# A decode block on one core: w1 in one transfer, w2 in four pieces in place of three

## The chip, the cores and the metric

The kernel runs on one core of a Trainium2 chip. The metric is device time in microseconds (us); lower is better. The core has five engines that run side by side: PE (TensorE, matrix products; PEld is its weight loads), DVE (VectorE), ACT (ScalarE), POOL (GpSimd), and SP (SyncE), which here only issues transfers. The transfers are carried out by 16 DMA engines, and an engine that needs a transfer's data waits until all of it has landed.

## The reference

One token (B = 1, S = 1, D = 640) passes a transformer block whose layer norms are scaled, shifted and gated by a conditioning vector c. All arrays are float32.

```python
mod = silu(c) @ w_mod                      # six vectors of 640: sa, ca, ga, sb, cb, gb
h = layernorm(x) * (1 + ca) + sa
q = h @ wq                                 # 32 heads of 192
p = softmax(q k^T * 192**-0.5)             # k_cache: 32 heads x 8192 x 192
x = x + ga * ((p @ v_cache) @ wo)
h = layernorm(x) * (1 + cb) + sb
f = relu(h @ w1 + b1) ** 2                 # w1: 640 x 1536
x = x + gb * (f @ w2 + b2)                 # w2: 1536 x 640
```

The two caches make up nearly all of the bytes read; w1 and w2 are 3840 KB each.

## The kernel before

Everything big goes through one ring of three equal slots in the on-chip memory (`slot`, L97). In turn they hold a first bundle of small weights (wm0), then the chunks of the caches with wq and wo packed between them (`PLAN`, L50 to L85), and at the end three bundles of weights, each in a slot of its own: wm1 (the modulation weights for the second half), w1 and w2. `load(n)` (L206) asks for slot number n, and SP issues the transfers for it; SP waits at that place in its queue until the last reader of the slot's former content is done. The order of the instructions on each engine is that of the program text; no scheduler moves them.

The loop over the chunks (L363) multiplies keys by the query on DVE (L258), adds halves on POOL (L385), reduces to scores on DVE (L266), takes the softmax, and multiplies the values on PE (L307). At the end of each pass `load(n + 3)` (L410) asks for the slot that this chunk leaves. The last three passes so ask for wm1, w1 and w2. The slot for w2 is the one that the last chunk leaves; its last reader is the matmul of `attend` at L342.

How a bundle is cut into transfers is told by lists of column positions, one transfer from each to the next (L213 to L220):

```python
W1_CUT = (3 * FF, KB * FF)            # L44: blocks 0-2, 3-4 of 5
W2_CUT = (6 * D, 10 * D, 12 * D)      # L45: blocks 0-5, 6-9, 10-11 of 12
...
            for b in cuts:            # L218
                nc.sync.dma_start(chunk_t[n][:, a:b], src[:, a:b])
                a = b
```

A block of w1 is 32 rows of each of four groups of rows (1536 columns, 768 KB); there are KB = 5. A block of w2 is the same of w2 (640 columns, 320 KB); there are FB = 12. A transfer is a wait of its own: a matmul waits for the piece that holds its block.

After the loop come, in this order: the last heads' attention (L417 to L420); the modulation vectors from wm1 (`mod`, L183) with the gathering of the attention's result (`gather`, L347) between its blocks; the second layer norm on DVE and ACT, with the matmuls of the last gate (`gate`, L187; L194) put between its steps on PE; the transpose of its result to hT2 (L123, called at L432); the first product over the five blocks of w1:

```python
    for b in range(KB):               # L436
        for g in range(G):
            nc.tensor.matmul(pf[32 * g:32 * (g + 1), :FG], hT2[:, b], w1_t[:, b, FG * g:FG * (g + 1)],
                             start=(b == 0), stop=(b == KB - 1))
```

then bias, relu and square on DVE (L441 to L443) and their transpose to fT (L123, called at L444), two small DVE operations for the gated bias (L447, L448), the second product, of the same form, over the 12 blocks of w2 (L453), and on DVE the gate and the residual (L456, L457). SP stores the result (L458). In the trace every matmul of L438 and L453 shows as two instructions with a weight load each: 8 instructions for a block, 40 for w1, 96 for w2.

Of the kernel before, what the change touches and what calls it, by code (L numbers as in the profile page):

```python
# [14 lines left out]
D = 640  # L15
# [3 lines left out]
FF = 1536  # L19
# [3 lines left out]
KB = DG // 32  # L23
# [17 lines left out]
VPC = 5  # L41
LEAD_FROM = 1300
LEAD = 120
W1_CUT = (3 * FF, KB * FF)  # L44
W2_CUT = (6 * D, 10 * D, 12 * D)  # L45
WM_CUT = (KB * D + 9 * D, KB * D + 15 * D)
EPS = 1e-5

# [40 lines left out]
def block_kernel(ctx: ExitStack, tc: tile.TileContext, kv, wm0, wm1, w1, w2, out):  # L89
# [7 lines left out]
    def slot(name):  # L97
        return strm.tile([P, SLOT], F32, tag="slot", name=name, bufs=3)
# [107 lines left out]
    def load(n):  # L206
# [5 lines left out]
        else:  # L212
            name, src, cuts = (("wm1_t", wm1, WM_CUT), ("w1_t", w1, W1_CUT), ("w2_t", w2, W2_CUT))[n - len(PLAN)]  # L213
            chunk_t[name] = slot(name)
# [286 lines left out]
```

## Time and profile before

| what | value |
|---|---|
| median of three runs | 1055.79 us (1055.74 to 1055.89) |
| the profiled execution | 1055.83 us |
| its span, first to last instruction | 1054.0 us |
| busy: DVE, PE, POOL, ACT | 830.2, 497.1, 188.2, 43.5 us |
| read from memory | 451.8 MB, 429 GB/s over the span |
| mean granted clock of PE | 0.718 of full speed |
| w1, two transfers: size, time from issue to landing | 2304 KB, 20.5 us; 1536 KB, 23.8 us |
| w2, three transfers: size, time from issue to landing | 1920 KB, 16.6 us; 1280 KB, 19.2 us; 640 KB, 20.3 us |

The times are read from the start of the span. What lies around the span (1.8 us) is start and end of the program. A time from issue to landing contains the time behind the transfers that were queued before. Idle time in the profile is put down to what ended it, written as `<-` and the engine, tile and line waited for.

### The profile page before, as it was taken

The numbers are of one execution on the slowest core, as the hardware profiler recorded it, in microseconds if no ns is written. First come the engines' busy times: TensorE is split into PE (matmuls) and PEld (weight loads), VectorE is DVE, ScalarE is ACT, GpSimd is POOL, SyncE is SP. The second block draws the span as 40 slices with busy tenths as digits, with TensorE's granted clock in tenths as the row PEclk, the third lists the DMA queues.
The fourth block names the chain that finished last, engine by engine and source line by source line (L and its number), as shares of the span: only waits on it lengthen the run. The fifth ranks groups of instructions, "written<-read, shape, count | busy, mean of one in ns | idle before, by whom it ended". The sixth has DMA issues, their size and how long they took to land.

```text
span 1054.0 us, 5116 instructions
## 1 busy us (share of the span) xinstructions
PE 497.1 (47%) x2100; PEld 133.9 (13%) x2100; DVE 830.2 (79%) x428; ACT 43.5 (4%) x122; POOL 188.2 (18%) x57
## 2 busy tenths in 40 slices
PE   2253345565452364535354357344436346345286
PEld 1010011111110010101011011011001011011022
DVE  1798878877959969888797895999887977988822
ACT  1000000000000000000000000000000000000001
POOL 0212121121212202212121121122211211211200
PEclk9676576778666686668676577676677767768699
DMA  9999999999999999999999999999999999999997
GB/s 408 434 429 431 429 432 443 449 428 431 429 433 431 429 436 430 433 430 442 435 430 433 433 427 430 436 439 436 429 429 433 432 436 438 434 431 430 420 428 313
DMA packets 8960, 452.15 MB, mean 429 GB/s; under 512 B 997, under 2 KB 1001, under 8 KB 1129
## 3 DMA queue, kind: packets, MB, share of 16 engines
q1 hardware_dynamic: 8936, 451.83, 99.3%
q8 instruction: 16, 0.26, 0.1%
q14 instruction: 8, 0.06, 0.0%
HBM read 451.82 MB, written 0.00 MB: 429 GB/s over the span
## 4 chain that ended last, share of the span: by engine, by line
DMA 56%; DVE 30%; PE 12%; ACT 1%; issue 0%; SPq 0%; DVEq 0%
DMA chunk<-in_kv 53%; DVE chunk L258 16%; DVE sc L266 12%; PE ps_o L307 6%; PE ps_q L239 2%; DMA w_t<-in_w 2%; PE att_a L340 2%; DMA wm_t<-in_wm 1%; DVE os L321 1%; DVE om L319 1%; PE ps_mod L183 0%; PE att_a L342 0%; ACT p L290 0%; PE ps_mx L282 0%; DVE nm L284 0%
## 5 line engine op out<-in xcount | busy, mean ns | idle before, releaser
L258 DVE TENSOR_TENSOR chunk<-chunk,qb 128x8064 f32<-128x8064 f32 (+19 forms) x81 | 419.7, 5212 | 127.8 <-DMA chunk<-in_kv 122.5
L307 PE MATMUL ps_o<-chunk,p 128*32 128x512 f32 x1536 | 301.5, 747 | 70.3 <-DMA chunk<-in_kv 60.8
L266 DVE TENSOR_REDUCE sc<-chunk 128x25 f32<-128x4800 f32 (+21 forms) x109 | 333.9, 3097 | 0.4
L385 POOL TENSOR_TENSOR chunk<-chunk 128x1824 f32<-128x1824 f32 (+9 forms) x51 | 187.5, 3676 | 806.5 <-DVE chunk L258 578.5
L282 PE MATMUL ps_mx<-ident,mp 128*128 128x128 f32 x32 | 14.5, 452 | 346.8 <-DVE mp L280 346.8
L307 PEld LDWEIGHTS ps_o<-chunk,p 128*32 128x32 f32 x1536 | 68.2, 133 | 278.6 <-issue 193.1
L340 PE MATMUL att_a<-chunk,oT 128*32 128x512 f32 x96 | 65.1, 833 | 42.6 <-DVE oT L330 42.6
L239 PE MATMUL ps_q<-chunk,ln_h 128*128 128x512 f32 x110 | 66.6, 767 | 25.8 <-DMA chunk<-in_kv 25.8
L282 PEld LDWEIGHTS ps_mx<-ident,mp 128*128 128x128 f32 x32 | 5.6, 176 | 375.6 <-DVE mp L280 306.8
L290 ACT ACTIVATE p<-sc,nm 128x256 f32<-128x256 f32 x32 | 16.2, 508 | 649.6 <-DVE nm L284 649.6
L239 PEld LDWEIGHTS ps_q<-chunk,ln_h 128*128 128x128 f32 x110 | 26.7, 253 | 63.7 <-issue 34.6
L319 DVE TENSOR_TENSOR om<-ps_o,mask 96x512 f32<-96x512 f32 x32 | 21.6, 675 | 8.5 <-PE ps_o L307 8.5
L284 DVE TENSOR_REDUCE nm<-ps_mx 128x1 f32<-128x128 f32 x32 | 9.3, 292 | 19.5 <-PE ps_mx L282 19.5
L321 DVE TENSOR_REDUCE os<-om 96x64 f32<-96x512 f32 x32 | 21.8, 682 | 1.1
L340 PEld LDWEIGHTS att_a<-chunk,oT 128*32 128x32 f32 x96 | 12.2, 142 | 78.1 <-DVE oT L330 45.1
L329 DVE TENSOR_REDUCE oT<-ps_oT 128x3 f32<-128x96 f32 x16 | 4.0, 248 | 21.0 <-PE ps_oT L325 21.0
L295 PE MATMUL ps_sum<-ident,wide 128*128 128x128 f32 x16 | 7.4, 465 | 22.4 <-ACT wide L293 22.4
L183 PE MATMUL ps_mod<-wm_t,silu 128*32 128x320 f32 (+1 forms) x80 | 9.4, 621 | 15.8 <-DVE silu L171 15.7
L325 PE MATMUL ps_oT<-ident,os 96*128 96x96 f32 x16 | 5.0, 313 | 20.8 <-DVE os L321 20.8
L342 PE MATMUL att_a<-chunk,oW 128*96 128x384 f32 x32 | 14.6, 538 | 0.0
L240 ACT ACTIVATE qb<-ps_q 128x512 f32<-128x512 f32 x12 | 7.2, 597 | 137.2 <-PE ps_q L239 137.2
L338 ACT ACTIVATE oW<-oT 128x96 f32<-128x96 f32 x16 | 4.5, 280 | 177.6 <-DVE oT L330 177.6
(78 smaller groups left out, 93.6 us busy)
## 6 DMA issues: line engine op xcount, KB each, us to landing
chunk<-in_kv SPq DMA_DIRECT2D x38, 8064.0 KB, 37.2
chunk<-in_kv SPq DMA_DIRECT2D x11, 8000.0 KB, 39.0
chunk<-in_kv SPq DMA_DIRECT2D x2, 7872.0 KB, 38.5
chunk<-in_kv SPq DMA_DIRECT2D x1, 6144.0 KB, 27.9
wm_t<-in_wm SPq DMA_DIRECT2D x1, 4493.5 KB, 13.9
wm_t<-in_wm SPq DMA_DIRECT2D x1, 4480.0 KB, 27.6
chunk<-in_kv SPq DMA_DIRECT2D x1, 3264.0 KB
chunk<-in_kv SPq DMA_DIRECT2D x1, 3072.0 KB, 28.2
```

The costliest lines, as they stand in the source:

```text
L183: nc.tensor.matmul(ps[32 * g:32 * (g + 1), :n * DG], e[:, b:b + 1].to_broadcast([P, 32]), wb[:, :, DG * g:DG * (g + 1)], start=(b == 0), s ...
L239: nc.tensor.matmul(ps, h1[:, b:b + 1].to_broadcast([P, P]), w[:, b], start=(b == 0), stop=(b == KB - 1))
L258: nc.vector.tensor_mul(pr, pr, q[:, None, :].to_broadcast([P, b - a, DH]))
L266: nc.vector.tensor_reduce(sc[:, a % SRING:a % SRING + b - a], src[:, a - first:b - first], axis=AX.X, op=ALU.add)
L282: nc.tensor.transpose(ps[:, :P], mp.to_broadcast([P, P]), ident)
L290: nc.scalar.activation(p, s[:, :, None].to_broadcast([P, NPOS, 32 // E]), AF.Exp, bias=nm, accum_out=sp[:, h % 2:h % 2 + 1])
L307: nc.tensor.matmul(ps_t[h][32 * g:32 * (g + 1)], p[:, E * j:E * (j + 1)].rearrange("p e r -> p (e r)"), t[:, g], start=(j == 0), stop=last)
L319: nc.vector.tensor_mul(om[:n], ps_t.pop(h)[:n].rearrange("p (d e) -> p d e", e=E), mask[:n, None, :].to_broadcast([n, ED, E]))
L321: nc.vector.tensor_reduce(os_[:n, h % 2], om[:n], axis=AX.X, op=ALU.add)
L340: nc.tensor.matmul(att_a[96:, :512], oT[:, j:j + 1].to_broadcast([P, 32]), w[:, j, :512], start=(first and j == 0), stop=(last and j == NV ...
L342: nc.tensor.matmul(att_a[:96, :NV * (D - 512)], oW.rearrange("p j r -> p (j r)"), w[:, :, 512:], start=first, stop=last)
L385: nc.gpsimd.tensor_add(half, half, kt[:, m:, DH // 2:])
```

## The change

Two lists of cuts change and nothing else. w1 comes in one transfer of five blocks (3840 KB) in place of three and two blocks. w2 comes in four transfers, of six, three, two and one block (1920, 960, 640 and 320 KB), in place of six, four and two. The order of the bytes in the queue stays as it was, and so does the number of transfers, five.

```diff
-W1_CUT = (3 * FF, KB * FF)
-W2_CUT = (6 * D, 10 * D, 12 * D)
+W1_CUT = (KB * FF,)
+W2_CUT = (6 * D, 9 * D, 11 * D, 12 * D)
```

## The prediction

> **What bounds the kernel now.** I read the page first, for what runs all the time. Rows two and three of this fence are the busy share of the DMA engines and what they moved, in 40 slices of 26 us; the last is the chain of work that ended last, by engine.
>
> ```profile
> span 1054.0 us, 5116 instructions
> ...
> DMA  9999999999999999999999999999999999999997
> GB/s 408 434 429 431 429 432 443 449 428 431 429 433 431 429 436 430 433 430 442 435 430 433 433 427 430 436 439 436 429 429 433 432 436 438 434 431 430 420 428 313
> ...
> DMA 56%; DVE 30%; PE 12%; ACT 1%; issue 0%; SPq 0%; DVEq 0%
> ```
>
> The DMA engines are at nine tenths in every slice but the last. The kernel is a stream of bytes, and the change neither adds nor removes a byte. So only the end of the stream can matter, and I go to the chain in order of time there (start, us, what).
>
> ```profile
> 1027.86 0.83 PE att_a L342 x2
> 1028.69 0.02 issue
> 1028.71 0.33 SPq L219
> 1029.04 0.05 issue
> 1029.09 0.43 SPq L219
> 1029.51 0.05 issue
> 1029.56 20.33 DMA w_t<-in_w
> 1049.89 0.04 issue
> 1049.93 0.80 PE ps_y L453 x16
> 1050.73 0.02 issue
> 1050.75 0.34 DVE y L456
> 1051.11 0.33 DVE y L457
> ```
>
> The slot for w2 comes free when L342 has read its last chunk; SP then issues the three pieces of w2, and the last of them lands at 1049.89. From there 0.04 us pass to the first matmul that uses it, 16 matmuls follow (two blocks), then two DVE operations and the store. **The landing of the last byte sets the end**, and 0.84 us lie between it and L456. Next, the timeline of the last steps (start, us, engine, line, tiles, count, and in brackets the idle time before with what ended it).
>
> ```profile
> 1036.97 1.30 PE L194 MATMUL ps_mod<-wm_t,silu 128*64 128x320 f32 x8
> ...
> 1038.49 0.34 DVE L123 STREAM_TRANSPOSE hT<-ln_h 128x160 f32<-128x160 f32 x1
> 1038.91 0.19 PEld L438 LDWEIGHTS ps_f<-w_t,hT 128*32 128x32 f32 x8 [1.20 <-PE ps_mod L194]
> 1038.94 3.43 PE L438 MATMUL ps_f<-w_t,hT 128*32 128x384 f32 x40 [0.67 <-PE ps_mod L194]
> ...
> 1040.71 0.32 PEld L438 LDWEIGHTS ps_f<-w_t,hT 128*32 128x32 f32 x8 [0.32 <-DMA w_t<-in_w]
> ...
> 1042.43 0.56 DVE L441 TENSOR_TENSOR f<-ps_f,bbt 128x384 f32<-128x384 f32 x1 [3.59 <-PE ps_f L438]
> ...
> 1044.01 0.58 DVE L123 STREAM_TRANSPOSE fT<-f 128x384 f32<-128x384 f32 x1
> ...
> 1044.83 0.33 DVE L448 TENSOR_TENSOR x<-x,gb 128x160 f32<-128x160 f32 x1
> 1045.37 1.54 PEld L453 LDWEIGHTS ps_y<-w_t,fT 128*32 128x32 f32 x48 [3.70 <-issue]
> 1045.40 1.84 PE L453 MATMUL ps_y<-w_t,fT 128*32 128x160 f32 x48 [3.03 <-DMA w_t<-in_w]
> 1048.38 0.97 PEld L453 LDWEIGHTS ps_y<-w_t,fT 128*32 128x32 f32 x32 [1.46 <-DMA w_t<-in_w]
> 1048.38 1.29 PE L453 MATMUL ps_y<-w_t,fT 128*32 128x160 f32 x32 [1.14 <-DMA w_t<-in_w]
> 1049.93 0.43 PEld L453 LDWEIGHTS ps_y<-w_t,fT 128*32 128x32 f32 x16 [0.58 <-DMA w_t<-in_w]
> 1049.93 0.75 PE L453 MATMUL ps_y<-w_t,fT 128*32 128x160 f32 x16 [0.26 <-DMA w_t<-in_w]
> ```
>
> A block of w2 is 8 matmuls here (48 for six). All three pieces of w2 are waited for, so PE has time to spare there. The second piece of w1 is waited for by a weight load at 1040.71, but the row of the matmuls is one run without a gap: that wait costs nothing today.
>
> **The change part by part.**
>
> *Issue.* SP issues one transfer less for w1 and one more for w2. The first is worth nothing, because SP then waits for L342 until 1028.71 anyway. The second comes at about 1030.0, one step of 0.43 + 0.05 us behind the last of before. Its cover is w1: in the order of the queue w2's bytes come only when w1's are in, at 1040.7. Without that 10 us cover it would cost 0.48 us.
>
> *Bytes.* PE's restarts tell when pieces land: 1280 KB take 1048.38 - 1045.37 = 3.01 us, 640 KB take 1049.93 - 1048.38 = 1.55 us. So 640 KB more cost 1.46 us (2.28 us per 1000 KB), and 1.55 - 1.46 = 0.09 us is the price of a transfer as such. Three blocks (960 KB) then take 2.28 us, and one block (320 KB) 0.82 us. The lower end for one block is half of the 1.55 us (0.78), the upper end the whole 1.55, as if size no longer counted. I take 0.82, near the lower end, since 1280 to 640 KB nearly halved. w2's tail becomes 2.28 + 1.55 + 0.82 = 4.65 us in place of 4.56, and w1 gives the same 0.09 back for its removed transfer: the last byte stays at 1049.89, and the pieces are usable at about 1045.37, 1047.65, 1049.2 and 1049.93. The transfers number five as before, so the waits at the kernel's end do not grow.
>
> The Trainium skill's page "DMA: Bandwidth & Descriptors", section "Bandwidth", speaks against such cuts: make transfers of at least 1 MiB to reach three quarters of the peak. Here 640 KB came in 1.55 us, 423 GB/s against 435 for the 1280 KB, so the trace does not bear it out behind a full queue.
>
> *The wait for w1.* L438 starts on a whole w1. The weight load that waits today goes at 1040.71, and 0.03 us later matmuls start (1038.91 to 1038.94 is the same step now), so 1040.74 in place of 1038.94: **1.80 us later**. Behind it on PE stand only L438's and L453's matmuls; behind L438 stand DVE's f, its square and its transpose. The 3.43 us of matmuls end at 1044.17, and fT is ready at 1044.59 + 1.80 = 1046.39. L447 and L448, next on DVE, end at 1046.96 in place of 1045.16, and L457 needs them at about 1051: hidden with 4 us to spare. From DVE's end to PE's first matmul I take 0.2 us, a little above the nearest step (fT's twin before L438, whose transpose of 0.34 us starts at 1038.49: 0.11 us); 0.1 would be the lower end, 0.5 a generous upper one. L453 starts at 1046.6 instead of 1045.40. This is the price of the edit, and it falls into the 1.84 us of work followed by 1.14 us of idle that L453 has today.
>
> *The pace of L453.* Four matmuls run side by side. From 16 to 48 matmuls the run grows from 0.75 to 1.84 us: 1.09 us for 8 groups of four, 0.136 a group, and a block is two groups. From 1046.6, blocks 0 to 5 take until 1048.23 (three blocks are there since 1047.65, no wait), blocks 6 to 8 until 1049.05 (wait to 1049.2), blocks 9 and 10 until 1049.77, and **the last block starts when it lands, 1049.93**. PE has caught up with 0.16 us in hand.
>
> *The end.* Behind the last landing stands one block in place of two: 0.75 - 2 x 0.136 = 0.48 us. That is 0.27 us less, and L456, L457 and the store move with it. Nothing else is late.
>
> **Sum:** the profiled execution took 1055.83 us (span 1054.0 and 1.83 us around it), less 0.27 is 1055.56. It lies 0.04 us over the median of 1055.79, so the forecast is **1055.5 us**, 0.03% less. That is far inside 0.2% (2.1 us), about what a measurement of this kernel can tell from no change. By its own unknowns: if the last piece came 0.16 us or more earlier, PE would be the bound and the gain 0.43 (1055.4); if one block took 1.55 us, the end is 0.73 later (1056.25).
>
> **The rivals.**
>
> *Slower: the clock of PE falls in the new gap.* PE now rests from the end of L194 to L438 and again from there to L453. These are stretches of this execution (window, its length, busy time and count of PE, PEld, DVE, ACT, POOL, then granted clock, DMA share, GB/s):
>
> ```profile
> 968.60:982.60 14.00, 0.48 (x1) 0.18 (x1) 11.99 (x5) 0.60 (x2) 4.04 (x1) 0.63 0.99 429
> 982.60:985.60 3.00, 2.95 (x12) 0.77 (x15) 2.97 (x1) 0.00 (x0) 0.00 (x0) 0.50 1.02 441
> ...
> 1042.40:1045.40 3.00, 0.00 (x0) 0.03 (x1) 2.59 (x6) 0.00 (x0) 0.00 (x0) 1.00 0.99 416
> 1045.40:1047.30 1.90, 1.84 (x48) 1.52 (x48) 0.00 (x0) 0.00 (x0) 0.00 (x0) 1.00 0.62 254
> ```
>
> After 14 us with 0.48 us of work the clock was at half for at least the next 3 us of work; after 3.0 us with none it was full. The new gaps are 1038.27 to 1040.74 (2.5 us) and 1044.17 to 1046.6 (2.4 us), both shorter than the one that did no harm, so this is unlikely. If it came, L438's 3.43 us would double, L453 would start at 1050.0, and its 24 groups (23 x 0.136 + 0.35 = 3.5 us) would end at 1053.5 where now 1050.68 stands: **1058.6 us**. It decides as soon as PE is over 0.16 us late. The Trainium skill's page "TensorE: Matmul & The Clock Gate", section "Why this matters for your kernels", advises against rests over about 3 us between bursts; by it the old gap was at the edge and the new ones are under it, which agrees with the rows.
>
> *Small transfers have a price that the old sizes hide.* One block takes the 1.55 us of two: **1056.25 us**. The fence on L453 speaks against it, as 1280 and 640 KB scale; below 640 KB no row of w2 shows it. The Trainium skill's page "DMA: Bandwidth & Descriptors", named above, points this way.
>
> *PE becomes the bound.* If L453's start is 0.3 to 0.9 us later than reckoned, the catching up fails, and 0.14 to 0.74 of it is seen: **1055.7 to 1056.25 us**. Then the change does not do what it says: the last cut no longer decides.
>
> *The latest DMA engine changes.* The 16 engines do not finish together; the windows, with DMA share and GB/s as their last columns:
>
> ```profile
> 1040.00:1045.00 5.00, 2.37 (x32) 0.82 (x24) 2.43 (x6) 0.00 (x0) 0.00 (x0) 1.00 0.98 413
> 1045.00:1048.00 3.00, 1.84 (x48) 1.54 (x48) 0.15 (x1) 0.00 (x0) 0.00 (x0) 1.00 0.63 260
> 1048.00:1050.00 2.00, 1.36 (x36) 1.00 (x40) 0.00 (x0) 0.00 (x0) 0.00 (x0) 1.00 0.17 69
> ```
>
> In the last 2 us 17% of them work, and a piece is usable when the latest is done. Program code comes through the same engines, by the page's row of that queue (packets, MB, share of 16 engines):
>
> ```profile
> q8 instruction: 16, 0.26, 0.1%
> ```
>
> 0.1% of 16 x 1054 us is some 17 us, 1.05 us for each packet. If such a packet moved onto or off the latest engine, the end would move by 1.05: **1056.6 or 1054.5 us**. The program's length hardly changes, which speaks against it.
>
> **How the numbers follow.** Forecast 0.72; small transfers dear 0.10; PE the bound 0.06; another latest engine 0.08; half clock 0.04. The range 1055.0 to 1056.4 holds the first three (0.88) with the forecast's own ends of 1055.4 and 1056.25; the width beyond these is for the 0.15 us by which the three runs differ, and an earlier landing by part of a code packet. Slower by over 0.2% is the half clock, 0.04. For faster by over 0.2% no case is left; I keep 0.02 taken from the forecast, for what the trace does not show. Within 0.2%: 0.94.
>
> **What would show it.** In the changed trace L438's first matmul starts at 1040.7 and its 40 run in 3.4 us; fT is ready near 1046.4; L453 starts near 1046.6, not behind a DMA; its last 8 matmuls wait for w2 at about 1049.9 and end 0.48 us later; L456 starts near 1050.5. It is wrong if the last matmuls follow their forerunners without waiting for a DMA (PE is the bound), if the last landing is over 0.3 us from 1049.9, or if the granted clock is below 1.00 after 1038 us.

## The result, and the profile after

| | median | single times | runs |
|---|---|---|---|
| before | 1055.94 us | 1055.62 to 1056.21 | 17 |
| after | 1056.99 us | 1055.65 to 1060.28 | 17 |

The ratio is 1.0016, with a 95% interval from 1.0008 to 1.0023: the change makes the kernel slower, by less than the 0.2% of the prediction's bound, and its median lies above the forecast's range. The medians say less than the single times do. Those of before lie within 0.6 us. Those of after fall into groups: two at 1055.7, seven from 1056.6 to 1057.0, six from 1058.1 to 1058.7, and 1059.8 and 1060.3. The two best are as good as before; the others lose about 1, 2.5 or 4 us.

The profiled execution took 1058.43 us, span 1056.7, and so belongs to the third group. This is its chain of work that ended last, in order of time (start, us, what), to be set beside that of before.

```profile
1014.78 25.71 DMA w_t<-in_w
1040.49 0.14 issue
1040.63 5.16 PE ps_f L438 x40
...
1047.39 0.58 DVE fT L123
1047.97 0.21 DVE gb L447
1048.19 0.04 issue
1048.23 5.12 PE ps_y L453 x96
1053.35 0.02 issue
1053.37 0.34 DVE y L456
```

The chain no longer goes through w2's landing. It goes from w1's landing through both products on PE, and L453 is one run of 96 matmuls. Its issues of w1 and of w2's last piece (KB, us to landing) show that the transfers came as forecast:

```profile
w_t<-in_w SPq DMA_DIRECT2D x1, 3840.0 KB, 25.7
...
w_t<-in_w SPq DMA_DIRECT2D x1, 320.0 KB, 19.8
```

The first landed at 1014.78 + 25.71 = 1040.49. The timeline has w2's four issues in one row, from 1028.70 to 1030.45:

```profile
1028.70 1.75 SPq L219 DMA_DIRECT2D w_t<-in_w  x4
```

An issue takes some 0.43 us, so the last one stood at about 1030.0, and 19.8 us later its data was there: 1049.8, as before. PE was at work until 1053.35. Its two products in the timeline:

```profile
1040.63 5.12 PE L438 MATMUL ps_f<-w_t,hT 128*32 128x384 f32 x40 [2.46 <-DMA w_t<-in_w]
...
1048.23 5.08 PE L453 MATMUL ps_y<-w_t,fT 128*32 128x160 f32 x96 [2.48 <-DVE gb L447]
```

L438 took 5.12 us in place of 3.43, for the same 40 matmuls without a wait inside. The windows view says why (window, length, busy time and count of PE, PEld, DVE, ACT, POOL, then granted clock of PE, DMA share, GB/s). The windows are cut at the borders, 3.41 us apart, at which the clock changes if it does:

```profile
1034.51:1037.92 3.41, 2.37 (x16) 1.28 (x16) 1.90 (x9) 0.26 (x1) 0.00 (x0) 1.00 0.96 408
1037.92:1041.33 3.41, 0.95 (x14) 0.40 (x16) 0.74 (x3) 1.18 (x4) 0.00 (x0) 1.00 0.91 385
1041.33:1044.74 3.41, 3.41 (x28) 1.48 (x24) 0.00 (x0) 0.00 (x0) 0.00 (x0) 0.50 0.99 412
1044.74:1048.15 3.41, 1.01 (x12) 0.16 (x4) 2.23 (x5) 0.00 (x0) 0.00 (x0) 1.00 0.67 271
1048.15:1051.57 3.42, 3.34 (x52) 2.86 (x56) 0.35 (x2) 0.00 (x0) 0.00 (x0) 0.50 0.07 27
1051.57:1053.40 1.83, 1.74 (x52) 1.39 (x44) 0.03 (x1) 0.00 (x0) 0.00 (x0) 1.00 0.00 0
```

Read the clock column downward: 1.00, 1.00, 0.50, 1.00, 0.50, 1.00, each for 3.41 us (the last row stops where PE stops). A window in which PE was busy for 0.95 us (28%) is followed by one at half clock; so is the next with 1.01 us (30%). In the window at half clock at most 28 matmuls of L438 ran, those that a border cuts counted with them, where 40 had taken 3.43 us. Now the same time in the execution of before. Its clock does not change here, so the borders are counted on from the last change, at 1006.39, in steps of 3.413 us:

```profile
1037.11:1040.53 3.42, 2.75 (x28) 1.16 (x31) 1.36 (x5) 1.41 (x5) 0.00 (x0) 1.00 1.01 424
1040.53:1043.94 3.41, 1.84 (x24) 0.60 (x16) 1.44 (x3) 0.00 (x0) 0.00 (x0) 1.00 0.97 410
1043.94:1047.35 3.41, 1.84 (x48) 1.54 (x48) 1.15 (x4) 0.00 (x0) 0.00 (x0) 1.00 0.79 325
```

Its rest of 3.0 us (1042.4 to 1045.4) fell across the border at 1043.94, so that each of the two windows beside it was 54% busy, and the clock stayed up.

**Theory CLOCK:** the clock of PE is decided window by window of 3.41 us, by the share of the window in which PE works; the borders fall differently in each execution; the change puts two rests of 2.5 us on a path that has next to no slack left (0.16 us by the prediction). **Rival SMALL:** small last transfers are dear. **Rival LATE:** PE cannot catch up even at full clock, because it starts L453 too late.

### The profile page after: what moved, and what is told of

It reads as the page before. It is cut to its first block, busy times and chain, and to the rows that moved or that the text cites. A ratio compares the mean times of both kernels' runs of the same rounds, so it can differ in the third digit from the quotient of the medians.

```text
span 1056.7 us, 5116 instructions
## 1 busy us (share of the span) xinstructions
PE 498.0 (47%) x2100; PEld 136.1 (13%) x2100; DVE 830.2 (79%) x428; ACT 43.5 (4%) x122; POOL 188.1 (18%) x57
## 4 chain that ended last, share of the span: by engine, by line
DMA 56%; DVE 30%; PE 12%; ACT 1%; issue 0%; SPq 0%; DVEq 0%
DMA chunk<-in_kv 53%; DVE chunk L258 16%; DVE sc L266 12%; PE ps_o L307 5%; PE ps_q L239 3%; DMA w_t<-in_w 2%; PE att_a L340 2%; DMA wm_t<-in_wm 1%; DVE os L321 1%; DVE om L319 1%; PE ps_mod L183 1%; PE ps_f L438 0%; PE ps_y L453 0%; ACT p L290 0%; PE ps_mx L282 0%
## 5 line engine op out<-in xcount | busy, mean ns | idle before, releaser
L307 PE MATMUL ps_o<-chunk,p 128*32 128x512 f32 x1536 | 293.2, 729 | 68.1 <-DMA chunk<-in_kv 58.6
L340 PE MATMUL att_a<-chunk,oT 128*32 128x512 f32 x96 | 68.6, 874 | 43.0 <-DVE oT L330 43.0
```

The source lines that it names most:

```text
L307: nc.tensor.matmul(ps_t[h][32 * g:32 * (g + 1)], p[:, E * j:E * (j + 1)].rearrange("p e r -> p (e r)"), t[:, g], start=(j == 0), stop=last)
L340: nc.tensor.matmul(att_a[96:, :512], oT[:, j:j + 1].to_broadcast([P, 32]), w[:, j, :512], start=(first and j == 0), stop=(last and j == NV ...
```

## The experiments

Each kernel ran 11 times; the times of before beside them are those of the same calls. The intervals of these ratios are about 0.1% to either side, 1 us, so verdicts rest on medians, on the spread of the single times and on the traces.

**Half of the change: w1.**

```diff
-W1_CUT = (3 * FF, KB * FF)
+W1_CUT = (KB * FF,)
```

> Only w1 in one transfer; w2 stays in pieces of six, four and two blocks. Theory CLOCK (PE's clock is halved when a stretch of about 3.4 us is mostly idle, the new rests before and after L438 do that in some executions, and the kernel has no slack left to hide it): median 1056.5 to 1058.5 us with single times spread from 1055.8 to about 1060, and in the profile either a granted clock of 0.50 in L438 or L453, or an end within 0.3 us of before. Rival SMALL (the loss comes from w2's smaller last pieces): within 0.2 us of before and no spread. Rival LATE (PE cannot catch up even at full clock): a steady 0.3 to 0.9 us over before, no spread.

Measured: median 1056.75, ratio 1.0013 (1.0004 to 1.0022), five times from 1055.73 to 1055.96, one of 1056.75, five from 1058.42 to 1059.60. Its profiled execution took 1059.02 us, with both products stretched:

```profile
1041.10 5.13 PE L438 MATMUL ps_f<-w_t,hT 128*32 128x384 f32 x40 [2.47 <-DMA w_t<-in_w]
1048.70 5.14 PE L453 MATMUL ps_y<-w_t,fT 128*32 128x160 f32 x96 [2.47 <-DVE gb L447]
```

In this execution the clock was 0.50 from 1042.22 to 1045.63 and from 1049.05 to 1052.46, after two windows that were 33% and 28% busy. Losses as large as those of after are there with w2's pieces as large as before: SMALL falls. LATE falls too, since it expected one steady loss. Only the group near 1056.7 is thinner here, one time of eleven against seven of seventeen.

**The other half: w2.**

```diff
-W2_CUT = (6 * D, 10 * D, 12 * D)
+W2_CUT = (6 * D, 9 * D, 11 * D, 12 * D)
```

> Only w2 in six, three, two and one block; w1 stays in two pieces. CLOCK: about 0.27 us less than before (one block of matmuls less behind the last landing), spread no more than that of before (0.6 us), with the half clock, where it falls into L453's first blocks, hidden by the waits for w2. SMALL: 0.5 us or more over before. LATE: as CLOCK, since L453 starts early.

Measured: 1055.73 (1055.24 to 1056.33) against 1055.82, ratio 0.9999 (0.9991 to 1.0008). The profile caught what the one of before had not: most of the rest before L453 (2.4 of 2.7 us) inside one window, and the half clock after it. Its windows:

```profile
1041.39:1044.81 3.42, 1.03 (x16) 0.17 (x6) 2.23 (x5) 0.00 (x0) 0.00 (x0) 1.00 0.99 414
1044.81:1048.22 3.41, 3.10 (x48) 2.65 (x52) 0.36 (x2) 0.00 (x0) 0.00 (x0) 0.50 0.66 267
```

and the timeline of the same execution:

```profile
1045.12 5.05 PE L453 MATMUL ps_y<-w_t,fT 128*32 128x160 f32 x96 [2.71 <-DMA w_t<-in_w]
1049.69 0.16 PEld L453 LDWEIGHTS ps_y<-w_t,fT 128*32 128x32 f32 x8 [0.21 <-DMA w_t<-in_w]
1050.24 0.32 DVE L456 TENSOR_TENSOR y<-ps_y,mods 128x160 f32<-128x160 f32 x1 [5.04 <-PE ps_y L453]
```

96 matmuls at full clock would take 3.5 us by the prediction's pace, so L453 took some 1.5 us longer, which is what 3.1 us at half clock cost. The kernel was still early (L456 at 1050.24; 1055.24 us in all), because L453 starts at 1045.1 and would only have waited for w2: its last weight loads still waited for the last piece, at 1049.69. Two things came out otherwise than expected. The median lies 0.09 us under before, not 0.27, and the times spread over 1.1 us, more than the 0.6 expected. A later run of this kernel with its rest filled (below) is nearer to both.

**No rests.** Matmuls whose result nobody reads are put into the two rests; nothing else in the text of the kernel changes:

```diff
+    def keep(n, name, cols=512):
+        ps = psum.tile([P, 512], F32, tag="sm", name=name, bufs=2)
+        for _ in range(n):
+            nc.tensor.matmul(ps[:, :cols], ident, qb[:, :cols], start=True, stop=True)
+
+    keep(2, "ps_keep1", 512)
...
+    keep(2, "ps_keep2", 512)
```

The first call stands before the loop of L438, the second behind it.

> The changed kernel with two extra matmuls of 128x512 without use (ident times the first 512 columns of qb, into a PSUM tile nobody reads) before L438 and two before L453's wait; they only keep PE busy for about 1.7 us of each rest. CLOCK: granted clock 1.00 from about 1033 us to the end, L438 in 3.4 us, single times within 0.6 us of each other, median 1055.5 to 1055.8. SMALL and LATE: as slow as the changed kernel's better runs, 1056.2 or more; the extra matmuls help nothing.

Measured: 1055.68, all eleven from 1055.28 to 1055.94; before 1055.82; ratio 0.9998 (0.9989 to 1.0006). The profiled execution took 1055.51 us. The windows view of its last part, the timeline of its products, and the end of its chain (the lines of L438, L453 and L456 are L444, L460 and L463 here, and L438 is the extra matmul):

```profile
1033.00:1053.00 20.00, 15.11 (x172) 7.49 (x168) 7.01 (x21) 1.44 (x5) 0.00 (x0) 1.00 0.71 295
```

```profile
1038.15 1.98 PE L438 MATMUL ps_keep<-qb,ident 128*128 128x512 f32 x4
1040.71 3.43 PE L444 MATMUL ps_f<-w_t,hT 128*32 128x384 f32 x40 [0.57 <-DMA w_t<-in_w]
1044.07 1.98 PE L438 MATMUL ps_keep<-qb,ident 128*128 128x512 f32 x4
1046.61 3.75 PE L460 MATMUL ps_y<-w_t,fT 128*32 128x160 f32 x96 [0.56 <-DVE gb L454]
```

```profile
1030.12 19.72 DMA w_t<-in_w
1049.84 0.04 issue
1049.89 0.52 PE ps_y L460 x8
1050.41 0.02 issue
1050.43 0.34 DVE y L463
```

With more work on PE the kernel is faster than the changed one (1055.68 against 1056.99). The clock is 1.00 throughout, and the chain runs through w2's landing again, with 8 matmuls behind it. This is the execution that was forecast.

**The same in before.**

```diff
+    keep(3, "ps_keep2", 512)
```

The call stands between L438 and L453, behind the same helper `keep`.

> The kernel before with three such matmuls between L438 and L453 (about 2.6 of 3.0 us of rest). CLOCK: no change within 0.15 us, because the waits for w2's pieces hide a half clock there. If it is faster by over 0.3 us, the kernel before was losing time to its clock as well.

Measured: 1055.84 (1055.53 to 1056.20) against 1055.82, ratio 1.0000 (0.9991 to 1.0009). So the rest of 3 us does not move the median of the kernel before. That it never costs it anything is not shown: of the 104 single times of before on record, six lie from 1056.42 to 1056.83, while the five kernels whose long rests were filled (55 executions, those of further down included) have none above 1056.20 but one far off. No trace caught such an execution of before.

**Which rest.** The filled kernel with only the first, then only the second filling.

> The changed kernel with the two extra matmuls without use before L438 only. CLOCK: only the rest before L453 can halve the clock, which costs about 1.2 us where the stretches of 3.4 us fall badly: about half of the times near 1055.6, the others near 1056.8, none above 1057.5; L438 takes 3.4 us. If the loss came from the rest before L438 alone: all near 1055.6. If it came from the second alone: as the changed kernel, up to 1058 and more.

> The changed kernel with the two extra matmuls between L438 and L453 only. CLOCK: only the rest before L438 can halve the clock, and what L438 then takes longer (up to 1.7 us) is seen at the end less some 0.4 us: about half of the times near 1055.6, the others near 1056.8, none above 1057.5. If the second rest alone were the cause: all near 1055.6.

Measured: with the first rest filled 1056.71, four times from 1055.42 to 1055.81 and seven from 1056.69 to 1057.31; with the second filled 1056.87, three from 1055.44 to 1055.70, six from 1056.63 to 1057.01, and 1057.83 and 1057.99, two more than expected above 1057.5. Ratios 1.0005 (0.9996 to 1.0014) and 1.0008 (0.9999 to 1.0016). Either rest alone costs about 1.3 us in more than half of the executions, and losses above 2.5 us were seen only where both rests were open, but for one execution at 1069.90 us (below). In the profile with the first rest filled the second one decides:

```profile
1043.94:1047.35 3.41, 0.93 (x30) 0.88 (x30) 2.59 (x6) 0.00 (x0) 0.00 (x0) 1.00 0.78 313
1047.35:1050.76 3.41, 3.41 (x60) 3.41 (x53) 0.00 (x0) 0.00 (x0) 0.00 (x0) 0.50 0.20 78
```

and with the second filled, the first:

```profile
1038.47:1041.89 3.42, 1.40 (x18) 0.65 (x20) 0.72 (x3) 1.18 (x4) 0.00 (x0) 1.00 0.96 406
1041.89:1045.30 3.41, 3.41 (x25) 1.35 (x20) 0.00 (x0) 0.00 (x0) 0.00 (x0) 0.50 0.97 399
```

There the rest was 2.02 us long:

```profile
1040.72 5.13 PE L443 MATMUL ps_f<-w_t,hT 128*32 128x384 f32 x40 [2.02 <-DMA w_t<-in_w]
```

The last pair of windows moves the bound up: one that was busy for 1.40 of 3.42 us, 41%, is followed by the half clock as well.

**How much filling.** One matmul in each rest (`keep(1, ...)`), and two of 16 columns (`keep(2, ..., 16)`).

> The changed kernel with one extra matmul (about 0.9 us) in each of the two rests in place of two. By the profiles so far full clock was lost after stretches of 3.41 us in which PE was busy less than about 0.42, that is, idle over 2.0 us. One matmul leaves 1.5 us of each rest, so CLOCK with that bound expects granted clock 1.00 from 1033 us on and all times within 0.6 us of each other, median 1055.5 to 1055.8. If the clock asked for less idle time than that (1.5 us or below), the spread up to 1058 stays.

> The changed kernel with the same number of extra matmuls as the filled one, two in each rest, but of 16 columns in place of 512 (some 0.3 us in all for each rest). CLOCK: the rests stay over 2 us, so the times spread like those of the changed kernel, 1055.6 to 1058.5 or more, with a median somewhat lower at most. If the extra instructions as such help (an earlier fetch, another order of waits): as the filled kernel, 1055.7 with no spread.

Measured, one matmul: 1055.67, all from 1055.42 to 1055.87, ratio 0.9998 (0.9989 to 1.0007). What is left of the rests, 0.54 and 1.42 us in the profiled execution, does no harm. Measured, 16 columns: median 1056.71, none under 1056.19, three from 1058.37 to 1059.63 (and one execution far off, at 1917 us, which no trace explains); ratio 1.0011 (1.0002 to 1.0020). So it is PE's time at work that counts, not the number of instructions. Its windows warn against taking the busy column for an exact measure:

```profile
1036.82:1040.23 3.41, 1.82 (x13) 0.97 (x12) 1.36 (x5) 1.44 (x5) 0.00 (x0) 1.00 0.94 394
1040.23:1043.64 3.41, 3.08 (x20) 1.15 (x24) 0.00 (x0) 0.00 (x0) 0.00 (x0) 0.50 0.96 403
```

The first looks 53% busy and the clock fell after it, though 54% was enough in before. Without the four tiny instructions, which show as 0.62 us, it would be some 37%. Whether tiny matmuls count less than their time in the profile was not tested: other windows from 41 to 54% busy, without any, went both ways (last section).

**Each half at full clock.** w1 alone with both rests filled, and w2 alone with its rest filled.

> Only w1 in one transfer (w2 in six, four and two blocks as before), with two extra matmuls without use in each of the two rests. CLOCK: no spread, and the same as before within 0.15 us (about 1055.85), since two blocks stand behind the last landing as before. If joining w1 has a price of its own at full clock: 0.3 us or more over before.

> Only w2 in six, three, two and one block (w1 in two pieces as before), with three extra matmuls between L438 and L453, so that the clock stays up there. CLOCK: no spread beyond that of before, 0.27 us less than before (about 1055.55), and a little less than the same kernel without the extra matmuls, where a half clock in L453 sometimes reaches the last blocks. If the last cut brings nothing: 1055.85.

Measured: w1 alone 1055.92 against 1055.92 for before (ten of eleven from 1055.59 to 1056.20, one at 1069.90, whose mean granted clock was 0.585 in place of about 0.72 and which no trace explains); ratio 1.0011 (0.9987 to 1.0036), an interval that this one time makes wide. w2 alone 1055.56 (1055.27 to 1055.92), ratio 0.9997 (0.9988 to 1.0006). Joining w1 has no price at full clock, and the last cut of w2 moves the median by 0.36 us. That kernel has the lowest median of all; the interval of its ratio does not part it from before, and its gain is shown by the medians and by the traces. From w2's last landing to the gate on DVE 0.59 us pass in its profiled execution, with 8 matmuls between (1050.03 to 1050.62), and 0.86 us in that of w1 alone with both rests filled, with 16 (1050.21 to 1051.07): the 0.27 us that the prediction forecast.

## Why the prediction was wrong

- **What bounds the kernel: right.** The end of the stream of bytes sets the end as long as PE keeps up; the last landing stayed where it was (about 1049.8). In the profiled execution of after PE did not keep up, and its last matmuls, which end at 1053.35, set the end.
- **Bytes and small pieces: right.** The filled kernel's last landing is at 1049.84 (forecast 1049.89). The rival of dear small transfers fell with w1 alone, where the loss is there without them.
- **The wait for w1: right.** L438 began at 1040.63 and 1040.71 (forecast 1040.74), L453 of the filled kernel at 1046.61 (1046.6), the last 8 matmuls at 1049.89 (1049.93), L456 at 1050.43 (1050.48). The profiled execution took 1055.51 us where 1055.5 was forecast. That it agrees to 0.01 us is luck: the filled kernel's times run from 1055.28 to 1055.94, with a median of 1055.68. (By the prediction's own pace blocks 9 and 10 end at 1049.74, not 1049.77; nothing hangs on it.)
- **The step that failed is the weighing of the first rival, the half clock, at 0.04.** The prediction compared the new rests of 2.5 and 2.4 us with one of 3.0 us "that did no harm" and took length for the measure. What counts is the share of work in windows whose borders differ in each execution. The old rest was cut by a border in the one execution profiled. A rest of 2.5 us is long enough when it falls well inside a window: 0.95 of 3.41 us busy, then 0.50. So two terms of the sum, both taken at full clock, were too small: L438 took 5.12 us in place of 3.43, and L453 5.08 in place of 3.81. And where the clock does fall after the old rest, L453 can take it out of its waits for w2, as the trace with w2 alone shows for one position of the border.
- **The hidden cost was read as no cost.** The prediction counted 0.16 us that PE would have in hand, and named that as the point from which the rival decides. It did not ask what the idle 1.14 and 0.26 us in L453's rows could cover in other executions. Joining w1 spent that cover.
- **The rival's price** was put at 1058.6 for a doubled L438 and a full-speed L453. The profiled execution stands at 1058.43, but that is luck, for it comes by other terms: against the forecast, -0.11 (start of L438), +1.69 (L438), +0.05 (to L453's start) and +1.27 (L453, 5.08 in place of 3.81) make 2.90, and the forecast L456 at 1050.48 becomes 1053.38 (measured 1053.37). The half clock lasts one window, not to the end, so neither product is doubled, and each rest can bring one such window. Hence groups in place of one price. The two slowest executions, about 4 us over before, were not caught in a profile; the traces account for losses up to 3.2 us.

The trace of before, from which the prediction took its two stretches, held the answer elsewhere. These are two windows in the middle of its span:

```profile
501.22:504.63 3.41, 1.15 (x3) 0.24 (x2) 0.00 (x0) 0.00 (x0) 0.00 (x0) 1.00 1.01 435
504.63:508.04 3.41, 1.98 (x9) 0.57 (x12) 2.00 (x1) 0.00 (x0) 0.00 (x0) 0.50 1.05 454
```

PE's last matmul before the border ended at 502.38, so its rest was 2.25 us old when the clock fell. That is shorter than either of the new rests.

## What to carry to other kernels

When a change moves waiting time from many short waits into one rest of PE, ask what clock the matmuls behind it will get, and whether they still have a wait to hide it in: here 136 of 2100 matmul instructions cost up to 4 us in single executions. One profile shows one position of the windows; a "rest that did no harm" in it may have been cut by a border or covered by a wait. Single times that fall into groups are the sign to look for, and a few idle matmuls in the rest were a cheap way both to test for it and to cure it.

## What the runs showed of the hardware

The granted clock changes only at borders 3.41 us apart, which lie differently in each execution (1037.92 and 1041.33 in the execution of after; 1041.39 and 1044.81 in that of w2 alone). In the windows shown here, one at full clock that was busy for 27 to 41% was followed by half clock and one of 54% was not; the one of 53% with tiny matmuls in it was. Half clock went back to full after windows that were 90% (3.08 of 3.41 us), 91%, 98% and 100% busy. The twelve traces of this case hold 1579 such windows at full clock: all 581 under 41% busy were followed by half clock, none of the 889 over 54% was, and of the 109 between them 21 were. The Trainium skill's page "TensorE: Matmul & The Clock Gate", section "Part 1: The HAM clock gate", has a free-running window of that length, which these borders agree with, and names an idle window as the cause of half rate. Here the measurement differs, and it decides: no window before these losses was idle, and rests of 2.0 to 2.5 us were enough. What decides between 41 and 54% was not settled; the busy share of the profile alone does not.
